# RWKV-style attention with a gated MLP: key transposes issued with the score matmuls, the early bonus on the score diagonal, u brought to channels by one transposition, and a new order table

## The chip, the cores and the metric

The kernel runs on one core of a Trainium2 chip. The metric is the time of one execution on the device in microseconds (us); less is better. Engines are named as in the profile: PE is the matmul engine (TensorE), PEld its weight loads, DVE is VectorE, ACT ScalarE, POOL GpSimd, and SP the engine that issues the DMAs. PSUM is the memory that PE writes to, in banks of 128 partitions by 512 floats.

## The reference

Batch 4, 8 heads, 768 steps, head size 48, all float32. A recurrent attention feeds a gated MLP:

```python
for t in range(S):                        # attention, state is [B, H, 48, 48]
    cur = einsum('bhd,bhe->bhde', u[None] * k[:, :, t], v[:, :, t])
    y[:, :, t] = einsum('bhd,bhde->bhe', r[:, :, t], state + cur)
    state = w[:, :, t][..., None] * state + einsum('bhd,bhe->bhde', k[:, :, t], v[:, :, t])
x = y.transpose(0, 2, 1, 3).reshape(B, S, 384)
h = maximum(x @ w_in, 0)                  # [4, 768, 1024]
u_, v_ = h[..., :512], h[..., 512:]       # v_ is normalised over its 512 columns
gated = u_ * (einsum('ts,bsd->btd', w_spatial, v_n) + b_spatial[None, :, None])
out = gated @ w_out                       # [4, 768, 384]
```

The term with u is called the bonus: step t adds v(t) times the sum over d of r(t,d) u(d) k(t,d), so it is a diagonal term of the score matrix.

## The kernel before

The attention is cut into 24 slots (4 batches by 6 chunks of 128 steps). A slot holds all 8 heads as 4 groups of two heads: head j of a group sits on partitions 64j to 64j+47, so tiles of k and r are 112 rows by 4x128 columns. A chunk has two halves of 64 steps, and the state S is carried from half to half. The steps of slot i:

- `slot_load` issues the DMAs of k, r (`kr`), w and v; `slot_prep` scales `kr` in place by products of w (scans on DVE) and makes the bonus values.
- `slot_a`: 16 score matmuls (L521), each on a 64x64 quarter of the PE array, into `paw`, two PSUM banks of which each half j of the heads has one; then a DVE `copy_predicated` (L525) puts the masked scores into the tile `AS`.
- `slot_kt`: k to time-major by 4 transpositions on the full array (L539, 112 rows by 128 columns each) into a bank of a pool of three ("pm"), and a copy of 128x448 from there to `KT` (L543, mostly on ACT).
- `slot_y`: matmuls of `AS` with v into two banks `py` (L556), and the same line with S and r.
- `slot_d`: 16 matmuls of KT with v per half (L612), on quarters of the array, into columns 256 to 447 of `paw`. The state update multiplies S on ACT (L637) or POOL and adds `paw` on DVE (L627, L625).
- `slot_x`: y is copied and added (L659, L661), transposed (L665), split in a high and a low part (L669, L672, L675) and so becomes `xT`, the MLP's input.

Bonus of the slots 0 to 5: PE makes the values per step and head (L415, `pg`), DVE multiplies v by them (L487, `bv`), and one full-array matmul with the identity starts `py` with that (L566). From slot 6 on, DVE and POOL make the values; three small copies (L493, `dgs`) and two writes (L501 on ACT, L503 on DVE or POOL) put them on the diagonal of `AS` before the scores are copied there.

The MLP multiplies in three float32r passes (high x high, high x low, low x high; L682 to L684): `ph` is x times the right half of w_in, `pu` times the left half, `pv` the mix over steps, `po` the last product. Its weights are converted by ACT and DVE as they arrive (L350, L355).

Nothing runs in the order in which it is written. Every operation is registered with `op`, and a long table of numbers (`PLAN`) gives each one its engine and a planned start; the operations are issued on each engine in the order of those starts. Lists named `hold` and `lim` give further order conditions that hold when such a table is made; they issue no instruction. While the table says that PE has a gap, before a certain operation, `fill` issues filler matmuls of a zero tile (L889, 128x128 float32, they add zero to `py`). Ten more stand at the end, while the last outputs are checked.

Of the kernel before, what the change touches and what calls it, by code (L numbers as in the profile page):

```python
# [16 lines left out]
C = 128  # L17
# [14 lines left out]
T2j S3j Tay Ad7 Ade S3oy S2on S5l Amk Voj Vqe Vse Axq Vzt Snc A1k8 V1ma V1qh V1t3 A1v4 G1y7 S9p A138 V15h V16q V1ac  # L32
A1gz V26o S2i S4k S8o Vh2 Tj4 Vax Vj2 Vk0 Vc6 Ve6 Veq Vfe Vky Vmm Ax2 Az7 V78 Vxk Tow Vu2 Tn2 Apq Tz9 T12f Tx1 V12s
A14u V1c0 T17r A19n V1cr T1eg A1fx T1he A1ig S1ao A2ar V2ep V2iz V2lm A2q1 V2ta Sod A1q3 V1s6 V1us V23b A25c V2hb S25b
A2ir V2kp V2na V2qo A2ve V2xs S3jg A40k G430 S15d A32n V3ol S4ch A4tr V4xq S2po A46i V4na S3yl A4uw V4wf S4gl A58z
V5cd S4ej A50e V51w S4ox A5i9 G5lb S2f5 A45d V4bs S57i A5xp G627 S58j A5jz G64u S4y2 A5el G5nz S2d2 A388 V3ae V3ca
V3ho A4bd V50c S2nm A3ar V4d3 V4ek V4g7 A4z9 V54h S2e3 V4b2 V4du V4hi V4l8 A52m V582 S47l V4ki V4mk V4z1 V55s A57t
V5b2 T1sb T21v T29d A2cd A2f4 A2fr S6m S7n Smb Guu T140 Vpg Vyv V11i Vvv Gy9 V12g V13i G12l G1dr A1ji A1oc V7u V1e2
T1kb V1n7 A1d3 T16b A1ap T1nc T1pg T1fg V1j7 A1lu V1p0 T1qq A1sw V1wg T1y5 A1zs T219 A28c T2cb T2e8 T2gl A2kc A2n8
A2t6 Sla Saq S14c V18n T1aq G1c6 V1h2 V1i9 V1fe V1i0 V1jx V1kl G1jc G1nd G21l A1wk V1xs T1w7 V21i A1x9 T1mg A1ro T1zh  # L40
T244 T1v5 V20s A21u V2ca T25d A27a V29a T2b9 A2e1 T2g4 A2ho T2l1 T2my T2ou A2ri A2v4 A2wu A2yv G2zm V3c3 V3hg V3iz
G3kn G3la G3lx A3rf A3z5 V40x A3od A3te G3xh V49s A4dl V4ol S12r S19o S1rd V250 T272 G1wm V28d G29g V1z3 G22e V2by
V2d0 G2bt V2fm A31x A2a2 V2am T2r3 V34l A2nj T2k5 A2m1 T2ii T37i T2sf V2wn A2zf V33u T38r A3d4 V3g5 T3hz A3jm T3l7
# [173 lines left out]
def kernel(  # L217
# [182 lines left out]
    def slot_prep(i):  # L400
# [72 lines left out]
        for n in range(2):  # L473
# [571 lines left out]
```

## Time and profile before

| | |
|---|---|
| median of 3 runs | 362.88 us (359.57 to 364.05) |
| profiled execution | 362.92 us, of which the span of the trace 361.1 us |
| mean granted TensorE clock | 0.991 of full speed |
| busy share of the span | PE 99%, PEld 92%, DVE 75%, ACT 58%, POOL 39% |
| chain of waits that ended last | PE 92%, DVE 4%, ACT 3% |
| DMA | 47.8 MB, mean 132 GB/s |

The trace is one profiled execution. A row of a timeline has a start and a duration, both in us from the start of the span. PE is pipelined: the recorded durations of consecutive matmuls overlap, so what a matmul costs in a full stretch is the distance from its start to the next start, not its duration. A float32 matmul leaves two records, so x32 is 16 matmuls. The granted clock is given in parts of full speed (2.4 GHz); 0.5 is the lower level, 1.2 GHz.

### The profile page before, as it was taken

Reading aid. Unit: us, or ns where it says so; the run is one execution under the profiler, and the core shown is the slowest. Engines: PE = TensorE matmul, PEld = TensorE weight load, DVE = VectorE, ACT = ScalarE, POOL = GpSimd, SP = SyncE. Lnnn points to the kernel's source line nnn. Section 1 sums busy time; section 2 is a strip of 40 time slices with the busy share of each in tenths; the row PEclk is TensorE's granted clock in tenths of the full one; section 3 lists DMA queues with packets and bytes.
Section 4 is the critical chain, followed back from the end, with each engine's and each line's share of the span. In section 5 each row is a group of like instructions: output and inputs, shape, how many; then the busy total and the mean of one; then the engine's idle time right before and its main releaser. Section 6 shows DMA issues by size and latency. Waiting matters only on the chain.

```text
span 361.1 us, 11353 instructions
## 1 busy us (share of the span) xinstructions
PE 356.2 (99%) x4656; PEld 331.1 (92%) x4656; DVE 271.3 (75%) x596; ACT 211.1 (58%) x587; POOL 141.1 (39%) x187
## 2 busy tenths in 40 slices
PE   7999999999999999999999999999999999999998
PEld 7987898899899989899999899899999888999997
DVE  8789998999999878999898697788565667333140
ACT  2357999896573777784454478783632296512212
POOL 1344357105544653526631267437335322223110
PEclk9978999999999999999999999999999999999999
DMA  7971976961554657634453643433545010000011
GB/s 201 262 224 56 274 247 178 287 220 49 147 142 132 209 159 230 174 84 149 144 159 118 186 146 117 121 99 107 142 129 168 1 25 2 22 23 0 24 65 71
DMA packets 21545, 47.80 MB, mean 132 GB/s; under 512 B 2545, under 2 KB 10354, under 8 KB 21490
## 3 DMA queue, kind: packets, MB, share of 16 engines
q1 hardware_dynamic: 21346, 46.85, 44.1%
q8 instruction: 37, 0.61, 0.7%
q14 instruction: 18, 0.15, 0.1%
q10 hardware_dynamic: 144, 0.20, 0.1%
HBM read 42.32 MB, written 4.72 MB: 130 GB/s over the span
## 4 chain that ended last, share of the span: by engine, by line
PE 92%; DVE 4%; ACT 3%; issue 1%; POOL 0%; DVEq 0%
PE pv L682 9%; PE pv L684 8%; PE pv L683 8%; PE py L556 7%; PE ph L682 5%; PE ph L684 5%; PE pu L682 5%; PE ph L683 5%; PE py L889 4%; PE pu L684 4%; PE po L682 4%; PE pu L683 4%; PE po L684 4%; PE po L683 4%; PE paw L521 4%; PE paw L612 3%
## 5 line engine op out<-in xcount | busy, mean ns | idle before, releaser
L682 PE MATMUL pv<-ws,vh 128*128 128x384 f32 x192 | 65.6, 342 | 0.0
L684 PE MATMUL pv<-ws,vl 128*128 128x384 f32 x192 | 64.3, 335 | 0.0
L683 PE MATMUL pv<-ws,vh 128*128 128x384 f32 x192 | 64.3, 335 | 0.0
L788 DVE TENSOR_TENSOR t<-pv,b_sb 128x384 f32<-128x384 f32 x32 | 17.6, 552 | 29.9 <-PE pv L684 29.9
L682 PEld LDWEIGHTS pv<-ws,vh 128*128 128x128 f32 x192 | 36.1, 188 | 0.5
L683 PEld LDWEIGHTS pv<-ws,vh 128*128 128x128 f32 x192 | 36.1, 188 | 0.2
L684 PEld LDWEIGHTS pv<-ws,vl 128*128 128x128 f32 x192 | 36.0, 188 | 0.0
L792 ACT CAST gh<-t 128x384 fp32r<-128x384 f32 x32 | 15.9, 509 | 32.2 <-DVE t L790 31.2
L682 PE MATMUL pu<-xT,wi 128*128 128x384 f32 x96 | 34.0, 354 | 0.1
L682 PE MATMUL po<-wo,gh 128*128 128x384 f32 x96 | 33.2, 346 | 0.0
L684 PE MATMUL pu<-xT,wi 128*128 128x384 f32 x96 | 32.4, 338 | 0.0
L684 PE MATMUL po<-wo,gl 128*128 128x384 f32 x96 | 32.3, 337 | 0.0
L683 PE MATMUL po<-wo,gh 128*128 128x384 f32 x96 | 32.3, 336 | 0.0
L683 PE MATMUL pu<-xT,wi 128*128 128x384 f32 x96 | 32.2, 336 | 0.0
L793 POOL TENSOR_TENSOR gl<-t,gh 128x384 fp32r<-128x384 f32 x14 | 14.7, 1053 | 44.4 <-ACT gh L792 44.2
L637 ACT ACTIVATE S<-S,prod 112x48 f32<-112x48 f32 x100 | 25.2, 323 | 9.3 <-DVE S L627 7.2
L711 ACT ACTIVATE hv<-ph 128x512 f32<-128x512 f32 x24 | 14.3, 594 | 27.7 <-PE ph L684 27.5
L682 PE MATMUL ph<-wi,xT 128*128 128x512 f32 x72 | 29.4, 409 | 0.0
L684 PE MATMUL ph<-wi,xT 128*128 128x512 f32 x72 | 28.3, 393 | 0.0
L683 PE MATMUL ph<-wi,xT 128*128 128x512 f32 x72 | 28.3, 392 | 0.0
L754 POOL TENSOR_TENSOR vl<-hv,vh 128x512 fp32r<-128x512 f32 x14 | 18.1, 1300 | 25.2 <-ACT vh L752 24.9
L779 ACT ACTIVATE us<-pu 128x384 f32<-128x384 f32 x32 | 15.1, 486 | 14.7 <-PE pu L684 14.6
(199 smaller groups left out, 964.7 us busy)
## 6 DMA issues: line engine op xcount, KB each, us to landing
kr<-in_tr_dram SPq DMA_DIRECT2D x24, 448.0 KB, 4.8
N<-in_nat_dram SPq DMA_DIRECT2D x18, 384.0 KB, 3.4
Nw<-in_gt_dram SPq DMA_DIRECT2D x16, 384.0 KB, 3.4
W<-in_tr_dram SPq DMA_DIRECT2D x24, 225.8 KB, 3.4
v<-in_nat_dram SPq DMA_DIRECT2D x24, 192.0 KB, 3.8
out_dram<-ot SPq DMA_DIRECT2D x18, 192.0 KB, 3.3
wst<-in_w_spT_dram SPq DMA_DIRECT2D x12, 192.0 KB, 4.9
out_dram<-ot SPq DMA_DIRECT2D x10, 96.0 KB, 3.5
```

What stands on the lines that cost most here:

```text
L521: nc.tensor.matmul(pa()[ks, j, g * L:(g + 1) * L], kr()[rs, 0, ts_], kr()[rs, 1, ts_], start=True, stop=True)
L556: nc.tensor.matmul(py()[row][L * a:L * (a + 1), D * n:D * (n + 1)], x, z, start=(a, row) not in started, stop=not left[0], skip_group_chec ...
L637: e.mul(S1[i % 2][a][:, g, :], S0[:, g, :], Wc[:, g:g + 1])
L682: nc.tensor.matmul(ps, ah, bh, start=first, stop=False)
L683: nc.tensor.matmul(ps, ah, bl, start=False, stop=False)
L684: nc.tensor.matmul(ps, al, bh, start=False, stop=last)
L754: lambda e, hv=hv, vh=vh, vl=vl: e.tensor_tensor(vl(), hv(), vh().bitcast(F32), ALU.subtract),
L779: op({"A": act(HT, True)}, lambda: nc.scalar.activation(us(), pu()[:, :HT], AF.Relu), r=[(pu, 0)], w=[(us, 0)])
L788: op({"V": dve(HT)}, lambda: nc.vector.tensor_tensor(t1(), pv()[:, :HT], b_sb[:, tsl], ALU.add), r=[(pv, 0), ("b", 0)], w=[(t1, 0)])
L792: op({"A": act(HT)}, lambda: nc.scalar.copy(gh(), t1()), r=[(t1, 0)], w=[(gh, 0)])
L793: op({"G": pool(HT), "V": dve(HT)}, lambda e: e.tensor_tensor(gl(), t1(), gh().bitcast(F32), ALU.subtract), r=[(t1, 0), (gh, 0)], w=[(gl, ...
L889: nc.tensor.matmul(pw, zk, zk, start=False, stop=True, skip_group_check=True)
```

## The change

1. The transpositions of k move into the score operation: after the 16 scores, 8 transpositions of 48 rows by 128 columns, one per group and head, write into columns 256 to 447 of the same two banks `paw`, which the state products of that slot overwrite later. The separate operation `slot_kt` is gone; KT is now 128x384. The score operation therefore waits also for the state adds of the slot before, which read those columns. The state products take 48 rows throughout.
2. Slots 0 to 5 get their bonus as the later ones do, by three copies and two writes on the diagonal of `AS`; `bv`, its matmul with the identity, two clearings of `AS` and one of `py` go.
3. u comes as 4x128 and is brought to channels by one transposition, not by 8 matmuls of one column.
4. The conditions in `hold` and `lim` go, the filler's start value changes, and the table is new. It has 58 fillers where there were 45.

```diff
 PLAN = """
-T2j S3j Tay Ad7 Ade S3oy S2on S5l Amk Voj Vqe Vse Axq Vzt Snc A1k8 V1ma V1qh V1t3 A1v4 G1y7 S9p A138 V15h V16q V1ac
+T1x9 S3j Thi Aik Aid S3n0 S4xw S5l Amk Vq8 Vsu Vwf Ayg G11s Spe A1l5 V1pd V1sw V1uw A1x6 V1yz Smb A15y V19x V1b6 V1ej
...
@@ slot_prep
-        if i < B_PE:
-            if i < AB:
-                op({"G": 0.5, "V": 0.3}, lambda e: e.memset(As(), 0.0), w=[(As, 0), (As, 1)], port=True)
-            bv = q["bv"] = buf(pm, [P, DM], "w3", f"bv{i}", W3)
-            op({"V": 0.56}, lambda: nc.vector.tensor_tensor(
-                bv().rearrange("p (h d) -> p h d", d=D), v().rearrange("p (h d) -> p h d", d=D),
-                dg()[:, :H].unsqueeze(2).broadcast_to([P, H, D]), ALU.mult), r=[(dg, 0), (v, 0)], w=[(bv, 0)])
-            return
@@ slot_a
+        pd = q["pd"] = buf(psA, [P, 2, 512], "pd", f"pd{i}", 1)
+        pd.make = lambda: paw
+        KT = q["KT"] = buf(p2, [P, 2, G * D], "KT", f"KT{i}", 1)
...
+            for g in range(G):
+                for j in range(2):
+                    rs = slice(64 * j, 64 * j + D)
+                    nc.tensor.matmul(pd()[:, j, G * L + g * D:G * L + (g + 1) * D], kr()[rs, 0, g * C:(g + 1) * C],
+                                     ident[rs, rs], is_transpose=True, start=True, stop=True)
...
-        op({"T": 0.53}, mm, r=[(kr, "k"), (kr, "r")], w=[(pa, 0)], mode="64x64")
+        op({"T": 0.73}, mm, r=[(kr, "k"), (kr, "r"), ("ds", i - 1)], w=[(pa, 0), (pd, 0)], mode="64x64")
+        op({"A": 0.53, "V": 0.56}, lambda e: (e.copy if e is nc.scalar else e.tensor_copy)(
+            KT(), pd()[:, :, G * L:G * L + G * D]), r=[(pd, 0)], w=[(KT, 0)])
@@ slot_kt
-            for g in range(G):
-                nc.tensor.transpose(pt()[:, g, :], kr()[:, 0, g * C:(g + 1) * C], ident[:R, :R])
-        op({"T": 0.317}, tp, r=[(kr, "k"), ("ds", i - 1)], w=[(pm_, 0)])
-        op({"A": 0.53, "V": 0.62},
-           lambda e: (e.copy if e is nc.scalar else e.tensor_copy)(KT(), pt()), r=[(pm_, 0)], w=[(KT, 0)])
@@ slot_y
-                nc.tensor.matmul(py()[0][:, :DM], ident, bv(), start=True, stop=False, skip_group_check=True)
-            op({"T": 0.67}, bonus, r=[(bv, 0)], w=[(py, 0)])
-        elif i == B_PE:
-            op({"V": 0.42}, lambda: nc.vector.memset(py()[0][:, :DM], 0.0), w=[(py, 0)])
@@ slot_d
-                    rows = slice(64 * j, 64 + j * D)
+                    rows = slice(64 * j, 64 * j + D)
...
-                        nc.tensor.matmul(pa()[rows, a, G * L + g * D:G * L + (g + 1) * D], KT()[ps, g, rows],
+                        nc.tensor.matmul(pa()[rows, a, G * L + g * D:G * L + (g + 1) * D], KT()[ps, j, g * D:(g + 1) * D],
                                          v()[ps, hs], start=True, stop=True)
@@ hv_unit
-        hold = lim["hv"][-4:-3]
...
-               r=[(xh, j), (xl, j)] + [("wv", k_, p) for p in range(2)] + (hold if k_ == 0 else []),
+               r=[(xh, j), (xl, j)] + [("wv", k_, p) for p in range(2)],
@@ fill
-        t = free = 1.1
+        t = free = 2.3
...
-                    warm(max(0.0, cold - 0.1) / 0.43 + max(0.0, o.start - max(b, COLD) - 0.1) / 0.224)
+                    warm(cold / 0.43 + max(0.0, o.start - max(b, COLD) - 0.1) / 0.224)
@@ u
-                nc.tensor.matmul(pu_()[64 * j:64 * j + D, g:g + 1], u_sb[:1, n * D:(n + 1) * D], ones[:1],
-                                 start=True, stop=True)
+    op({"S": 0.45}, lambda: nc.sync.dma_start(u4, gu[:G].rearrange("g p a -> g (p a)")), w=[("u4", 0)], dma=0.01)
+    op({"T": 0.1}, lambda: nc.tensor.transpose(pu_()[:, :G], u4, ident[:G, :G]), r=[("u4", 0)], w=[(pu_, 0)])
```

How the order of the instructions moves is shown at three places. Numbers behind a tile's name count buffers; an x behind a row counts equal neighbours.

PE at the start of the program, before (`py` from `zk` is the filler, `pu__` is u, `pg` the bonus values, `pt` the transposed k, `paw` the scores and the state products):

```order
L889 MATMUL py0_88<-zk_78 128x128 x7
L931 MATMUL pu__167<-few_97,u_sb_110 48x1 x8
L889 MATMUL py0_88<-zk_78 128x128 x5
L415 MATMUL pg0_192<-up_sb_111,rk0_184 128x2 x4
L889 MATMUL py0_88<-zk_78 128x128
L539 MATMUL pt0_207<-ident_92,kr0_144 128x112 x4
L889 MATMUL py0_88<-zk_78 128x128
L521 MATMUL paw_87<-kr0_144 64x64 x16
L889 MATMUL py0_88<-zk_78 128x128 x10
L612 MATMUL paw_87<-v0_154,KT0_235 64x48 x2
```

PE at the same place, changed:

```order
L852 MATMUL py0_88<-zk_78 128x128 x9
L890 MATMUL pu__171<-ident_92,u_sb_110 128x4
L852 MATMUL py0_88<-zk_78 128x128
L415 MATMUL pg0_177<-up_sb_111,rk0_160 128x2 x4
L852 MATMUL py0_88<-zk_78 128x128 x5
L516 MATMUL paw_87<-kr0_143 64x64 x16
L522 MATMUL paw_87<-ident_92,kr0_143 128x48 x8
L852 MATMUL py0_88<-zk_78 128x128 x8
L587 MATMUL paw_87<-v0_151,KT0_238 48x48 x16
L415 MATMUL pg1_275<-up_sb_111,rk1_246 128x2 x4
L852 MATMUL py0_88<-zk_78 128x128 x9
```

The transpositions now follow the scores at once, the copy to KT lies under 8 fillers, and the bonus values of slot 1 come before the outputs of slot 0.

PE in the middle of the program at slot 12, before (`ph` and `pu` are MLP products):

```order
L684 MATMUL ph1_5_2513<-wi0_122,xT1_1_1_2362 128x512
L539 MATMUL pt12_2535<-ident_92,kr12_2209 128x112 x4
L682 MATMUL pu1_1_0_2544<-xT1_1_0_2353,wi0_122 128x384
L683 MATMUL pu1_1_0_2544<-xT1_1_1_2362,wi0_122 128x384
L684 MATMUL pu1_1_0_2544<-xT1_1_0_2353,wi1_123 128x384
L521 MATMUL paw_87<-kr12_2209 64x64 x16
L612 MATMUL paw_87<-v12_2337,KT12_2550 64x48 x2
```

PE at slot 12, changed, the scores with what follows and then the state products with what stands around them:

```order
L659 MATMUL po0_1_2_2454<-wo0_126,gl0_1_3_1868 128x384
L516 MATMUL paw_87<-kr12_2250 64x64 x16
L522 MATMUL paw_87<-ident_92,kr12_2250 128x48 x8
L543 MATMUL py0_88<-v11_2230,AS1_86 64x48
...
L659 MATMUL pu1_0_3_2556<-xT1_0_0_1879,wi1_123 128x384
L587 MATMUL paw_87<-v12_2440,KT12_2543 48x48 x16
L640 MATMUL yt11_2594<-ident_92,y11_2551 128x128 x3
```

Before, the state products (L612) stand right behind the scores in 13 of the 24 slots, both on quarters of the array. Now the copy to KT has to come between them, so the state products stand by themselves between full-array matmuls, and the array changes its split more often: counted in the order of PE from the second transposition of y (of slot 1) to the end, 50 times before and 104 times in the change.

ACT near the start, before:

```order
L937 COPY up_sb_111<-pu__167 48x4 x2
L350 ACTIVATE e_('wv', 0)_203<-d_('wv', 0)_146 128x512
L543 COPY KT0_235<-pt0_207 128x448
L476 COPY vs0_270<-v0_154 64x192
L355 CAST wi0_122<-e_('wv', 0)_203 128x512
L476 COPY vs0_270<-v0_154 64x192
L350 ACTIVATE e_('wv', 2)_303<-d_('wv', 2)_156 128x512
L637 ACTIVATE S101_116<-S0_114,prod_131 112x48 x4
L659 COPY y0_337<-py0_88 128x384
```

ACT at the same place, changed:

```order
L893 COPY up_sb_111<-pu__171 48x4 x2
L485 COPY dgs0_186<-pg0_177 128x4
L350 ACTIVATE e_('wv', 0)_190<-d_('wv', 0)_145 128x512
L485 COPY dgs0_186<-pg0_177 64x4
L493 ACTIVATE AS0_85<-id64_105,dgs0_186 128x64 x4
L526 COPY KT0_238<-paw_87 128x384
L493 ACTIVATE AS0_85<-id64_105,dgs0_186 128x64 x4
L355 CAST wi0_122<-e_('wv', 0)_190 128x512
L476 COPY vs0_281<-v0_151 64x192
```

The copies and the writes on the diagonal of slot 0 (L485, L493) stand on ACT among the conversions of the weights, and those of slots 1 and 2 follow behind them in the same way.

## Rows read from the trace of the kernel before

**Rows 1.** The page: span, busy time of each engine, chain of waits by engine.
```profile
span 361.1 us, 11353 instructions
PE 356.2 (99%) x4656; PEld 331.1 (92%) x4656; DVE 271.3 (75%) x596; ACT 211.1 (58%) x587; POOL 141.1 (39%) x187
PE 92%; DVE 4%; ACT 3%; issue 1%; POOL 0%; DVEq 0%
```

**Rows 2.** Windows: busy of PE, PEld, DVE, ACT, POOL; PEclk, DMA share, GB/s.
```profile
25.00:30.00 5.00, 5.00 (x75) 4.11 (x75) 3.80 (x9) 3.89 (x11) 2.33 (x3) 0.61 0.13 51
30.00:60.00 30.00, 30.00 (x602) 25.14 (x595) 28.45 (x61) 27.24 (x77) 15.31 (x20) 1.00 0.68 202
```

**Rows 3.** Timeline of PE from its first filler to the transposition of y of slot 1.
```profile
2.34 3.35 PE L889 MATMUL py<-zk 128*128 128x128 f32 x14 [2.34 <-DVE py L279]
...
6.70 2.50 PE L889 MATMUL py<-zk 128*128 128x128 f32 x10
8.99 1.71 PE L415 MATMUL pg<-up_sb,rk 112*128 112x2 f32 x8
...
12.46 1.13 PE L521 MATMUL paw<-kr 48*64 48x64 f32 x32
13.53 3.32 PE L889 MATMUL py<-zk 128*128 128x128 f32 x20
...
32.64 0.55 PE L665 MATMUL yt<-ident,y 128*128 128x128 f32 x3
```

**Rows 4.** Timeline of DVE, slot 0's product of k and r.
```profile
6.94 0.67 DVE L410 TENSOR_TENSOR rk<-kr 112x512 f32<-112x512 f32 x1
```

**Rows 5.** Groups of ACT by line: busy us, mean ns of one, idle before.
```profile
L637 ACT ACTIVATE S<-S,prod 112x48 f32<-112x48 f32 x100 | 25.2, 323 | 9.3 <-DVE S L627 7.2 <-DVE S L625 2.0
L501 ACT ACTIVATE AS<-id,dgs 128x64 f32<-128x64 f32 x68 | 17.9, 337 | 3.4 <-DVE dgs L493 2.5 <-PE py L556 0.8
...
L543 ACT COPY KT<-pt 128x448 f32<-128x448 f32 x22 | 11.6, 528 | 12.5 <-PE pt L539 12.5
L476 ACT COPY vs<-v 64x192 f32<-64x192 f32 x27 | 9.4, 351 | 3.4 <-DMA v<-in_nat_dram 2.9
L659 ACT COPY y<-py 128x384 f32<-128x384 f32 x16 | 7.6, 476 | 7.6 <-PE py L556 7.5
...
L493 ACT COPY dgs<-dg 64x4 f32<-64x4 f32 x16 | 3.1, 192 | 1.8 <-DVE dg L467 1.6
```

**Rows 6.** Timeline of ACT, a conversion beside four state products.
```profile
26.57 0.67 ACT L350 ACTIVATE e_('wv', 1)_398<-d_('wv', 1)_212 128x512 f32<-128x512 f32 x1
27.14 0.99 ACT L637 ACTIVATE S<-S,prod 112x48 f32<-112x48 f32 x4
```

**Rows 7.** Timeline of PE, the bonus matmul of an early slot between its neighbours.
```profile
39.64 0.40 PE L682 MATMUL ph<-wi,xT 128*128 128x512 f32 x1
...
40.33 0.81 PE L566 MATMUL py<-bv,ident 128*128 128x384 f32 x2
40.97 0.55 PE L539 MATMUL pt<-ident,kr 112*128 112x112 f32 x4
```

**Rows 8.** Timeline of PE in the middle, around the scores of one slot.
```profile
199.20 0.33 PE L683 MATMUL pv<-ws,vh 128*128 128x384 f32 x1
199.37 0.34 PE L684 MATMUL pv<-ws,vl 128*128 128x384 f32 x1
199.64 0.26 PE L556 MATMUL py<-v,AS 64*64 64x48 f32 x2
...
200.61 0.66 PE L521 MATMUL paw<-kr 48*64 48x64 f32 x32
201.09 0.63 PE L612 MATMUL paw<-v,KT 64*64 64x48 f32 x32
201.65 0.60 PE L539 MATMUL pt<-ident,kr 112*128 112x112 f32 x4
202.02 0.42 PE L682 MATMUL pv<-ws,vh 128*128 128x384 f32 x1
```

More of the change, by code (lines that the diff above doesn't have):

```diff
@@ L600, in slot_d @@
         KT, v = q["KT"], q["v"]
-        pa = q["pd"] = buf(psA, [P, 2, 512], "pd", f"pd{i}", 1)
-        pa.make = lambda: paw
+        pa = q["pd"]
         subs = 1 if i % NC_ == NC_ - 1 else SUB
@@ L687 @@
     gg = {}
-    lim = {"hv": [], "out": []}
     def hv_unit(b, c):
@@ L739, in scale @@
         small({"V": 0.16, "G": 0.2}, lambda e: e.tensor_tensor(part(5), part(7), part(1), ALU.mult), 1, 7, 5)
-        for j, (hv, end) in enumerate(zip(hvs, done)):
+        for j, hv in enumerate(hvs):
             vh, vl = vn[b, h * NH + j] = tuple(
@@ L754, in scale @@
                lambda e, hv=hv, vh=vh, vl=vl: e.tensor_tensor(vl(), hv(), vh().bitcast(F32), ALU.subtract),
-               r=[(hv, 0), (vh, 0)], w=[(vl, 0), end], port=True)
+               r=[(hv, 0), (vh, 0)], w=[(vl, 0)], port=True)
     def g_unit(b, h, f):
@@ L770, in g_unit @@
                + ([(us, 1)] if k_ == 0 else []), w=[(pu, 0)])
-        hold = [(vn[b, NC_ - 1][0], 0)]
-        if f > 0:
-            hold += lim["out"]
-        if f == KF - 1:
-            lim["out"] = []
-        if f == 0:
-            hold += [("wo", k_, 1) for k_ in range(KF)] if h else []
         op({"A": act(HT, True)}, lambda: nc.scalar.activation(us(), pu()[:, :HT], AF.Relu),
@@ L785, in g_unit @@
                 k_ == 0, k_ == NC_ - 1),
-               r=[(vh, 0), (vl, 0)] + [("ws", p, k_, h) for p in range(2)]
-               + (hold if k_ == 0 else []), w=[(pv, 0)])
+               r=[(vh, 0), (vl, 0)] + [("ws", p, k_, h) for p in range(2)],
+               w=[(pv, 0)])
         op({"V": dve(HT)}, lambda: nc.vector.tensor_tensor(t1(), pv()[:, :HT], b_sb[:, tsl], ALU.add),
@@ L803, in out_unit @@
                 po()[:, :DM], gh()[:, ts_], gl()[:, ts_], wo[0][:, f, :], wo[1][:, f, :], f == 0, f == KF - 1),
-               r=[(gh, 0), (gl, 0)] + [("wo", f, p) for p in range(2)]
-               + ([(gg[b, h, KF - 1][1], 0)] if f == 0 else []), w=[(po, 0), ("po", b, h, j)])
-        lim["out"].append(("po", b, h, j))
+               r=[(gh, 0), (gl, 0)] + [("wo", f, p) for p in range(2)],
+               w=[(po, 0)])
         op({"A": act(DM, True), "V": dve(DM)},
@@ L864, in general @@
             with tc.For_i(0, B, 1) as n:
-                lim["hv"], lim["out"] = [], []
                 prog.reset()
@@ L923 @@
     op({"T": 0.1}, lambda: warm(1), w=[("pw", 0)])
[L924 removed]
+    u4 = u_sb[:G, :P]
+    op({"S": 0.45}, lambda: nc.sync.dma_start(u4, gu[:G].rearrange("g p a -> g (p a)")), w=[("u4", 0)], dma=0.01)
     pu_ = buf(psM, [P, 512], "pm", "pu_", 3)
[L927 to L934 removed]
+    op({"T": 0.1}, lambda: nc.tensor.transpose(pu_()[:, :G], u4, ident[:G, :G]), r=[("u4", 0)], w=[(pu_, 0)])
     for j in range(2):
@@ L948 @@
             slot_w(i, 0)
-        slot_kt(i)
         slot_y(i)
```

190 lines of the change are left out of this document (86 added, 104 removed).

## The prediction

> **What bounds the kernel now.** I read the page first: PE is busy 99% of the span of 361.1 us and holds 92% of the chain of waits [rows 1]. Busy time alone would not prove it, since records of pipelined matmuls overlap, but the windows agree: from 30 to 60 us PE is busy for 30.00 of 30.00 us, while ScalarE has 27.24 and VectorE 28.45 [rows 2]. So from about 26 us on PE is issued without a gap, and what it is given to do sets the end; ScalarE and VectorE are close behind it as long as the attention runs. Before that, PE is carried along by fillers: its timeline from 2.34 us shows blocks of them between the first steps of the slots [rows 3], and there the other engines set the pace. I therefore read the start as a chain of waits, and the rest as a ledger of PE time by distances from start to start. The border is the second transposition of y (slot 1), at 32.64 us before [rows 3].
>
> The profiled execution took 362.92 us, 1.8 us over its span, and the median is 362.88; so the sum is made against 362.92 and needs no correction. About 2% (7.3 us: 355.6 and 370.1) is what a measurement of this kernel can tell from no change.
>
> **The start.** Fillers at first cost 3.35 / 7 = 0.48 us each, later ones 3.32 / 10 = 0.33 [rows 3]. In the changed order of PE: 9 fillers from 2.34 end at 6.7; u transposed, two tenths at most, 6.9; one filler, 7.4. The bonus values of slot 0 wait for the product of k and r, which VectorE ends at 6.94 + 0.67 = 7.6 [rows 4], and take 1.71 [rows 3]: 9.3. Five fillers, 11.7; scores 1.13 [rows 3], 12.9; the 8 transpositions at about half of that, 13.4. Eight fillers of 0.33 (2.7) cover the copy to KT, which costs ScalarE 0.53 [rows 5]: 16.1. State products 201.65 - 201.09 = 0.56 [rows 8], and the bonus values of slot 1 at 1.71 x 0.33 / 0.48 = 1.2: 17.8.
>
> From there ScalarE is the slow one, since it now writes diagonals among conversions. Up to the second transposition of y its order holds 4 groups of state products of 0.99 [rows 6] (4.0), 3 groups of diagonal writes of 4 x 0.337 less overlap (17.9 / 17 = 1.05 each [rows 5], 3.2), 6 copies of y, xT and KT at 0.48 to 0.53 (3.0), 4 copies of v at 0.35 (1.4), 5 conversions at 0.67 at most [rows 6] (3.3) and 6 small copies of 0.19 [rows 5] (1.1): 16.0. Neighbours overlap, 0.67 becoming 27.14 - 26.57 = 0.57 [rows 6]; a tenth for each of the 28 pieces would make it 13.3. I take 14.8, the middle: 32.6; then y's add on VectorE, half a us by the copy of the same shape (0.476 [rows 5]): 33.1. **Term 1: +0.5.** The transposition of u, the loads and the smaller set of clearings lie beside this and cost nothing; were they uncovered they could not move more than the 0.2 already counted.
>
> **The ledger from there on.**
> - **Term 2, moved ahead: -1.4.** Of the three MLP products of the first `ph` only one stood before the border; now all three do. One costs 40.33 - 39.64 = 0.69 [rows 7]; two of them, 1.4.
> - **Term 3, bonus matmuls: -2.6.** Four of six lie behind the border, at 40.97 - 40.33 = 0.64 [rows 7].
> - **Term 4, old transpositions: -7.8.** 21 slots at 202.02 - 201.65 = 0.37 [rows 8].
> - **Term 5, new transpositions: +5.0.** No row shows a transposition on half the rows. Bounds: if the two heads of a group run beside each other and only the 48 moving columns count, 4 x (0.37 / 4) x 48 / 112 = 0.16 a slot; if the eight run one after another at the old price of a load of 128 columns, 8 x 0.37 / 4 = 0.74. The nearest rows are the scores: 16 in 201.09 - 200.61 = 0.48 [rows 8], on the same rows of the array, straight ahead of them; two of those four quarters' columns make one such half, so a pair goes for two scores, 0.06. Four pairs: 0.24; times 21.
> - **Term 6, changes of the array's split: +4.9.** Behind the border the order has 54 more of them. From quarters to the full array costs 0.56 (state products with what follows) less 0.48 (scores with what follows) = 0.08; from full to quarters 199.64 - 199.37 = 0.27 less 199.37 - 199.20 = 0.17, so 0.10 [rows 8]. Bounds 0 (a change between halves and quarters may be free, none is shown) and 0.11; I take 0.09 for all. 54 x 0.09.
> - **Term 7, fillers: -1.0.** Three fewer behind the border, 0.33 each.
> - **Term 8, ScalarE behind the border: +1.0.** Slots 3 to 5 add to it one group of diagonal writes (1.05) and nine small copies (9 x 0.19 = 1.7), together 2.8, where it was idle for 30.00 - 27.24 = 2.76 [rows 2]. VectorE loses three products of v at about half a us and takes the other writes, about even. I put a third of the 2.8 on the path; bounds 0 and 2.8.
>
> The state products keep their number and lose only rows, which I price at zero: scores of 48 rows and 64 columns go at 0.48 for 16, state products of 64 rows at no more than 0.56 with the change of split behind them [rows 8]. Dropped conditions issue nothing. Sum: +0.5 - 1.4 - 2.6 - 7.8 + 5.0 + 4.9 - 1.0 + 1.0 = **-1.4**, so 362.9 - 1.4 = **361.5 us**. In words: what the removed operations give back, the split of the array takes again.
>
> **A rule that speaks against it.** The trace's old transpositions take 0.37 / 4 = 0.0925 each [rows 8]. The Trainium skill, "TensorE: Matmul & The Clock Gate", section "LDWEIGHTS", says that a load costs by its columns and not by its rows, P / 1.2 ns. By that, eight loads of 128 columns one behind the other would take 0.85 us a slot, and the sum would come out about 13 us higher; the trace's 0.0925 lies under the page's 0.107, and no row here shows two halves loaded side by side. The Trainium skill, "TensorEngine Tiling (Array Packing)", section "Key Properties", says that a change of tiling mode drains the engine; the 0.08 and 0.10 of rows 8 agree for quarters and full array, and no row shows halves against quarters.
>
> **Rivals.**
> - **R1, slower: the two halves do not run beside each other.** Then a slot pays 0.74 in place of 0.24, and 21 x 0.50 = 10.5 more: 372.0. It decides from 0.65 a slot on. For it: a load of 128 columns is the longest part of such a transposition, and PEld is busy 331.1 us [rows 1]. Against: scores with the same rows run four at a time. Chance 0.08.
> - **R2, faster: the split changes for nothing and pairs cost by their moving columns.** Minus 4.9, minus 21 x 0.08 = 1.7: 354.9. For it: the 0.08 and 0.10 are differences of single starts and may hold waits for operands. Against: they agree with each other. Chance 0.12.
> - **R3: ScalarE holds the attention up.** The start at 16.0 (+1.2) and all of the 2.8 on the path (+1.8): 364.5. For it: 27.24 of 30 us; against: VectorE and POOL take some of the writes, and PE has MLP work in hand. Chance 0.14.
> - **R4: the scores wait for the adds of the slot before**, since they now write their columns, and PE, which goes in order, stands with all MLP work behind them. If each of 21 slots stands for the length of a copy of 0.35 [rows 5], 7.3: 368.8. Against: the order puts MLP products between adds and scores. Chance 0.05.
>
> The forecast itself has 0.61, with a range of its own of 358.5 to 364.5 (terms 1, 6 and 8 at either bound move it by about 3). The granted clock was 0.61 from 25 to 30 us [rows 2]: at full speed elsewhere, that is 3.9 us at the lower level and 2 us of work lost; whether it comes again or goes lies within this range, since ScalarE sets that stretch. The range of 8 in 10 is 355.0 to 368.0: it leaves out R1 (0.08), half of R2 and of R4, and little else. Faster by over 2%: R2 and a tail, 0.13. Slower by over 2%: R1 and a tail, 0.09. Within: 0.78.
>
> **What would show it.** In the changed trace: eight transpositions 0.24 us from first start to the next operation's, less the change of split (term 5; 0.6 and more is R1); state products with about 0.1 to the neighbours on both sides (term 6; no gap is R2); the second transposition of y at 33 us (term 1); ScalarE without idle time between 18 and 33 us, and PE without a gap after 33 (a gap in front of scores is R4, one in front of matmuls of `AS` is R3). The forecast is wrong if the transpositions cost what the old ones did, or if PE is idle for more than 3 us in all behind the border.

## The result

The changed kernel takes 366.80 us in the median of 4 runs (364.94 to 369.47), the kernel before, run beside it, 362.56. The ratio is 1.0122, with a 95% interval of 1.0077 to 1.0167: slower by about 1%. The forecast was 361.5 us. Repeated twice, the comparison gave 1.0099 (1.0058 to 1.0140) and 1.0165 (1.0090 to 1.0239). All ratios here leave out runs more than 1.5% above the fastest run of the same kernel. The profiled execution took 365.9 us with a span of 364.2, 3.1 us more than the span before [rows 1].

The page of the changed kernel; the lines answer to rows 1:

```profile
span 364.2 us, 11570 instructions
PE 354.3 (97%) x4751; PEld 327.2 (90%) x4751; DVE 265.8 (73%) x585; ACT 224.9 (62%) x638; POOL 127.7 (35%) x174
PE 88%; ACT 7%; DMA 2%; DVE 1%; issue 1%; POOL 0%; DVEq 0%; ACTq 0%
```

PE is less busy and the span is longer, so time went where PE does nothing. The windows of the changed kernel, columns as in rows 2:

```profile
20.00:25.00 5.00, 5.00 (x53) 4.89 (x52) 1.50 (x4) 4.48 (x15) 1.74 (x2) 0.50 0.97 292
25.00:30.00 5.00, 5.00 (x120) 4.43 (x120) 5.00 (x10) 3.69 (x13) 3.70 (x3) 0.88 0.45 105
30.00:60.00 30.00, 28.84 (x535) 23.96 (x533) 27.31 (x62) 28.11 (x86) 11.09 (x18) 1.00 0.77 227
```

From 20 to 25 us the granted clock is 0.50, the lower level, and from 30 to 60 PE is idle for 1.16 us, where it had no gap before.

PE's timeline of the start; an "issue" in brackets is time in which the engine waited for nothing the profile shows:

```profile
17.18 0.50 PE L516 MATMUL paw<-kr 48*64 48x64 f32 x17
19.00 0.46 PE L516 MATMUL paw<-kr 48*64 48x64 f32 x15 [1.32 <-issue]
19.38 0.66 PE L522 MATMUL paw<-ident,kr 48*128 48x48 f32 x8
...
32.95 0.52 PE L640 MATMUL yt<-ident,y 128*128 128x128 f32 x3
```

In the middle of slot 1's scores PE stands for 1.32 us. The matmuls on either side are of one operation, so no other engine can be waited for; the clock falls at 19.4 us. ScalarE's timeline shows who waited for it:

```profile
16.05 2.01 ACT L493 ACTIVATE AS<-id,dgs 128x64 f32<-128x64 f32 x8
20.09 0.48 ACT L526 COPY KT<-paw 128x384 f32<-128x384 f32 x1 [2.02 <-PE paw L522]
```

Last, the end. These are the sequencer rows of the line with the last branch (past it lies the path for inputs out of range); behind the duration in ns (least, median, most) stands the start in us. First the changed kernel, then the kernel before:

```profile
L942 DVEq COMPARE_BRANCH  x1: 84/84/84, 359.4 to 359.4; - x1
L942 DVEq EVENT_SEMAPHORE  x1: 21/21/21, 363.2 to 363.2; - x1
```

```profile
L987 DVEq COMPARE_BRANCH  x1: 84/84/84, 358.3 to 358.3; - x1
L987 DVEq EVENT_SEMAPHORE  x1: 21/21/21, 358.9 to 358.9; - x1
```

VectorE's next instruction behind the branch comes 3.7 us later (359.48 to 363.17), where it had been 0.5. The span ends 1.0 us after the later of VectorE's instruction and PE's last matmul, so now 3.26 us behind that matmul (360.92), not 1.03 (360.07): 2.2 of the 3.1 us.

### The profile page after: what moved, and what is told of

Read it like the earlier page. It is cut to its first block, busy times and chain, and to the rows that moved or that the text cites. A ratio compares the mean times of both kernels' runs of the same rounds, so it can differ in the third digit from the quotient of the medians.

```text
span 364.2 us, 11570 instructions
## 1 busy us (share of the span) xinstructions
PE 354.3 (97%) x4751; PEld 327.2 (90%) x4751; DVE 265.8 (73%) x585; ACT 224.9 (62%) x638; POOL 127.7 (35%) x174
## 4 chain that ended last, share of the span: by engine, by line
PE 88%; ACT 7%; DMA 2%; DVE 1%; issue 1%; POOL 0%; DVEq 0%; ACTq 0%
PE pv L657 10%; PE pv L659 9%; PE pv L658 9%; PE py L543 6%; PE py L852 5%; PE po L659 4%; PE po L658 4%; PE po L657 4%; PE ph L657 4%; PE pu L657 4%; PE pu L658 4%; PE ph L659 4%; PE pu L659 4%; PE ph L658 4%; PE paw L516 4%; PE paw L587 3%
## 5 line engine op out<-in xcount | busy, mean ns | idle before, releaser
L657 PE MATMUL po<-wo,gh 128*128 128x384 f32 x96 | 32.4, 338 | 0.0
L658 PE MATMUL po<-wo,gh 128*128 128x384 f32 x96 | 32.3, 336 | 0.0
L612 ACT ACTIVATE S<-S,prod 112x48 f32<-112x48 f32 x84 | 21.2, 326 | 6.9 <-DVE S L602 6.8
L493 ACT ACTIVATE AS<-id,dgs 128x64 f32<-128x64 f32 x92 | 24.1, 339 | 0.2
L452 POOL TENSOR_TENSOR kr<-kr,F 112x496 f32<-112x496 f32 x16 | 18.0, 1126 | 13.4 <-DVE kr L442 11.7
L852 PE MATMUL py<-zk 128*128 128x128 f32 x116 | 19.9, 325 | 2.6 <-DVE py L279 2.3
```

The costliest lines, as they stand in the source:

```text
L452: op({"V": 0.68, "G": 1.07}, lambda e: e.tensor_tensor(seg(kr()[:, 0])[:, :, :L2 - 1], seg(kr()[:, 0])[:, :, :L2 - 1], F()[:, :, 1:].unsqu ...
L493: e.mul(As()[:, j, g, :], id64, dgs()[:, j, g:g + 1])
L612: e.mul(S1[i % 2][a][:, g, :], S0[:, g, :], Wc[:, g:g + 1])
L657: nc.tensor.matmul(ps, ah, bh, start=first, stop=False)
L658: nc.tensor.matmul(ps, ah, bl, start=False, stop=False)
L852: nc.tensor.matmul(pw, zk, zk, start=False, stop=True, skip_group_check=True)
```

## The experiments

**The same kernel again, without the branch, and with transpositions in quarters.** The first kernel is the changed one, unedited. In the next two, made of the changed kernel and of the kernel before, the branch, the hint that belongs to it and the slow path are left out:

```diff
-    rv = nc.values_load(bad[0:1, 0:1], min_val=0, max_val=1)
-    with tc.If(rv > 0, label="tail"):
-        general()
```

> The changed kernel once more, nothing edited. Three theories of its +3.0 us (profiled 365.9 against 362.9): (T) the tail, 2.2 us, since VectorE stood 3.7 us between the last branch and its next instruction where it had stood 0.5 before; (S) the changes of the array's split, which with the new transpositions cost 11.2 us where I had 9.9; (W) waits in which PE is idle, 1.7 us more behind the second transposition of y. If T belongs to the program, this trace shows the 3.7 us again and the ratio is 1.010 to 1.014; if T was chance, the last PE record ends at about 361 again but the span ends 1 us after it, and the ratio falls to 1.002 to 1.008. S and W expect the same PE sums as before within 0.3 us.

Measured: 1.0099; 3.3 us behind the branch again, the span 2.9 us behind PE's last matmul. So the tail belongs to the program. But the second transposition of y came at 35.28 us; PE had stood twice, 0.96 us at 18.2 us and then 2.05 us:

```profile
24.87 0.39 PE L543 MATMUL py<-S,kr 48*64 48x48 f32 x11
27.31 0.88 PE L543 MATMUL py<-S,kr 48*64 48x48 f32 x21 [2.05 <-issue]
```

> The changed kernel without the last branch and what lies behind it (the slow path for inputs out of range is left out; the check value is computed and not read). T expects the span to end 1 us after the last PE record, so 362 us, 364 in all, 2.2 less than the changed kernel; S and W expect no more than the branch's own 0.3 us to go.

> The kernel before, with the same branch and slow path left out. Its engines all passed the branch within 0.6 us and its end waits for PE's last fillers, so T expects 0 to 0.4 us less than the kernel before. Then the changed kernel without branch against this one shows the change without the tail: T 1.002 to 1.005, S and W as sole causes 1.012.

Measured, against the kernel before: the changed kernel 1.0066 (1.0039 to 1.0092) without the branch, the kernel before 0.9980 (0.9951 to 1.0009). Both spans end 0.9 to 1.2 us behind PE's last matmul. Between them the change is still 0.9% slower, where T alone wanted 0.2 to 0.5%: the tail is a part, not the whole. The traces of this pair agree: the second transposition of y is 1.6 us later (31.91 for 30.28), from there to PE's last product it takes 0.8 us more (326.15 for 325.32), and the end adds 0.3. Leaving the branch out took 2.4 us off the changed kernel's median (365.45 for 367.82, over all runs) and 0.3 off that of the kernel before (362.50 for 362.84). That is what T wants, but resampling the runs puts the 2.4 anywhere from -0.7 to 3.8 (95%), so the times alone do not prove it.

The fourth kernel has the transpositions in quarters:

```diff
             for g in range(G):
-                for j in range(2):
-                    rs = slice(64 * j, 64 * j + D)
-                    nc.tensor.matmul(pd()[:, j, G * L + g * D:G * L + (g + 1) * D], kr()[rs, 0, g * C:(g + 1) * C],
-                                     ident[rs, rs], is_transpose=True, start=True, stop=True)
+                for a in range(SUB):
+                    for j in range(2):
+                        rs = slice(64 * j, 64 * j + D)
+                        nc.tensor.matmul(pd()[a * L:(a + 1) * L, j, G * L + g * D:G * L + (g + 1) * D],
+                                         kr()[rs, 0, g * C + a * L:g * C + (a + 1) * L],
+                                         ident[rs, rs], start=True, stop=True)
```

> The changed kernel with the transpositions cut to quarters of the array: 16 products with the identity of 48 rows by 64 columns each, in the split in which the scores run, so that between scores and transpositions nothing changes. S expects the scores' sum behind the second transposition of y to fall from 13.3 back to 11.1 us (0.10 a slot), and the products to take 0.36 (scores' 0.48 by 48/64 columns) plus 0.08 for the change to the full array, 0.44 a slot for 0.38: a net of -0.9 us, ratio 1.009 to 1.011. If the longer score sum is not the change of split but waits for the columns of the slot before, it stays at 13.3 and the time rises by 1.3 us.

Measured: 1.0192 (1.0161 to 1.0224), a miss of the time; that ratio rests on three of six runs, and the median of all six is 373.57 us, 10.7 above the kernel before. Summed behind the border from start to next start, the scores fell as S said, to 10.6 us from 13.3, but the transpositions cost 10.5 for 7.95, 0.50 a slot where S had 0.44, so nothing was won or lost there. The rest is waits: the border came at 36.30 us for 32.95, and behind it PE waited 6.3 us for 2.85. PE stood inside one operation again, now at other places and longer; the longest stand lies ahead of the border:

```profile
26.44 0.61 PE L523 MATMUL paw<-ident,kr 48*64 48x48 f32 x26
31.02 0.38 PE L523 MATMUL paw<-ident,kr 48*64 48x48 f32 x6 [3.97 <-issue]
```

Counted in PE's records (loads, matmuls and semaphores), these stands lie in the changed kernel before records 449, 705, 1473, 1985 and 5569, in this one before 450, 962, 1729, 5058 and 9409: each within 1 of 449 plus a multiple of 256. A DMA queue that the profile calls "instruction" moves 38 packets of 16 KB, about one for every 256 of PE's 9,574 records, and PE goes on 2.3 to 2.8 us after the last of them has started (once 3.2). Both point to PE standing for its code, and a denser program, with 1,152 records more, stands longer; at most of the 36 such places of a trace it does not stand. Two waits that the profile puts down to nothing don't fit the count, 0.69 and 0.89 us before record 1448 in two kernels with clearings (below), at the start of a slot's scores; they too end 2.3 to 2.5 us after such a packet has started.

The Trainium skill, "Runtime: NRT & Kernel Launch", section "Instruction fetch mechanics", says that code is refilled in 16 KiB blocks of 256 instructions, and that crossing a block is mostly hidden. The trace agrees on the 256; that it is hidden holds for PE in the kernel before, whose four traces (two of them of its variants) show no such stand above 0.15 us (its variant with the bonus alone, below, has two), and fails for the changed kernel. At record 449 the clock may be part of the difference: those four traces reached the full clock only at 15.3 to 17.3 us (one had it for 3.4 us before), every trace with a stand there had it by 8 us, and the two kernels below that got it at 15.4 and 18.8 us have none. It isn't enough by itself, since two more below had it by 7.3 us and don't stand there.

**Where the last branch lies in VectorE's code.** Clearings of one element at about 348 us, where VectorE is idle; 16 or 40 of them in the changed kernel, 8 in the kernel before:

```diff
             nc.vector.tensor_tensor(okr[:, 0:1], okr[:, 0:1], okr[:, 1:2], ALU.min)
+            for _ in range(16):
+                nc.vector.memset(over[:1, :1], 0.0)
```

> The changed kernel with 16 one-element clearings more on VectorE, at about 348 us, where VectorE is idle; they only move the last branch in VectorE's code from its 704th instruction to the 720th. Theory T in its sharper form: where VectorE's last branch lies against the blocks in which code is loaded decides whether it stands 0.5 or 3.5 us behind it. T expects the 0.5 us back, the span to end 1.0 to 1.2 us after PE's last record, and 2 us less than the changed kernel: ratio to the kernel before 1.004 to 1.008. If the stall belongs to something else of the changed kernel (its work at the end, its outputs), it stays at 3.3 to 3.7 us and the ratio at 1.010 to 1.012.

> The kernel before with 8 such clearings, which put its last branch on VectorE's 704th instruction, as in the changed kernel. T expects VectorE to stand 3.3 to 3.7 us behind the branch here too, and 2 us more: ratio 1.005 to 1.006. The rival expects 0.5 us and a ratio of 1.000.

The rows of the branch, with 16 in the changed kernel, then with 8 in the kernel before:

```profile
L944 DVEq COMPARE_BRANCH  x1: 84/84/84, 361.1 to 361.1; - x1
...
L944 DVEq EVENT_SEMAPHORE  x1: 21/21/21, 361.7 to 361.7; - x1
```

```profile
L989 DVEq COMPARE_BRANCH  x1: 84/84/84, 358.8 to 358.8; - x1
...
L989 DVEq EVENT_SEMAPHORE  x1: 21/21/21, 362.6 to 362.6; - x1
```

The stall follows the position: 0.5 us with the branch as VectorE's 694th, 696th, 700th, 720th or 744th instruction, 3.2 to 3.7 as the 704th, in all seven traces that have it there, of either kernel and its variants. In those seven a second "instruction" queue, of 8 KB packets, moves one more packet 0.6 us after VectorE has gone on (at 363.76 us in the first); no other trace with the branch has one there. 704 is also the last number ahead of 449 plus 256, a place where PE stands; that VectorE's code is cut at the same numbers is not tested. The same section of the Trainium skill says that a taken branch whose target is not in the two blocks at hand stalls until it is loaded; the trace fits that, with 3.2 to 3.7 us as the price. The kernel before with the stall ran at 1.0036 (0.9992 to 1.0079), near the 1.005 expected, but no change is not excluded. The changed kernel without it ran at 1.0188 (1.0138 to 1.0237), which T does not explain, so it ran twice more:

> The changed kernel with the 16 clearings on VectorE once more. Its tail was 1.0 us as T wanted, but its time was 1.019 of the kernel before, where T alone wants 1.004 to 1.008; its trace showed PE without code for 1.25 us at 17.6 us and a granted clock of half for 10 us right behind, and again at 48.6 us (0.69 us) and half for 3.4 us behind. Theory C: PE's code comes in blocks of 256 instructions; where the changed kernel runs through one faster than the next arrives, PE stands, and a stand is followed by a stretch at the lower clock; how long both last differs from run to run. C expects 1.004 to 1.012 in the mean of more runs, and in this trace stands only at PE's instructions 449, 705, 961 and so on in steps of 256. If the 1.019 belongs to the program, it comes again.

> The changed kernel with 40 clearings on VectorE at about 348 us, so that its last branch is the 744th instruction. T expects 0.5 us behind that branch and, in the same call, 1.5 to 2.5 us less than the changed kernel: 1.004 to 1.008. If it comes out at 1.012 or above again, as the kernel with 16 clearings did, then what the tail saves is lost ahead of it, in the start.

> The changed kernel a third time, beside the next kernel on the same chip. Open: whether the 2 us of the tail, plain in every trace, are in the times, and how much of the rest is the start. T expects 1.010 to 1.012 here and 3.3 to 3.7 us behind VectorE's last branch; C expects PE to stand at its instruction 449 if the full clock came before 10 us, and a stretch at half behind it.

Measured: 1.0121, 1.0132 and, for the unshifted kernel, 1.0165. The first misses what C wanted of its trace too: no stand at 449, only the 0.89 us before record 1448. Pooled, 18 runs with the short tail and 19 with the long one have the same median, 367.6 and 367.7 us. In the three traces of each, the tail is 2.0 us shorter (1.02 for 3.08), but the last product of PE comes 2.2 us later (361.4 for 359.1), with a stretch at the lower clock at about 50 us in all three of the shifted kernels and in none of the three unshifted:

```profile
45.00:50.00 5.00, 4.63 (x96) 3.65 (x96) 4.96 (x13) 4.86 (x19) 1.76 (x3) 1.00 0.85 242
50.00:55.00 5.00, 5.00 (x42) 4.86 (x41) 4.34 (x11) 4.90 (x14) 2.27 (x4) 0.66 0.83 254
55.00:60.00 5.00, 5.00 (x87) 4.45 (x85) 3.60 (x9) 3.36 (x9) 2.13 (x8) 1.00 0.94 294
```

In two of the three PE also waits 2.21 and 1.63 us for xT at about 154 us (at most 0.37 in the unshifted). In VectorE's order the add for xT stands behind a reduction that waits for POOL; from the second trace with 16 clearings:

```profile
152.53 0.55 DVE L467 TENSOR_REDUCE dg<-N 128x8 f32<-128x384 f32 x1 [1.10 <-POOL N L465]
153.00 0.55 DVE L652 TENSOR_TENSOR xT<-yt,xT 128x384 fp32r<-128x384 f32 x1
153.61 0.50 PE L657 MATMUL ph<-wi,xT 128*128 128x512 f32 x1 [2.21 <-DVE xT L652]
```

Neither belongs to the clearings alone: without them, the changed kernel without branch waits 1.43 us for the same xT, and the kernel with seven operations on POOL (below) has a stretch at half at 53 us; the kernel with later loads (below) has the clearings and neither. What causes this loss stays open. That the tail holds 2 us of each trace is shown; that clearings which take it away make this kernel faster is not.

**Loads issued later.** The 16 clearings, and four words of the table (two parts of w_in, two of w_spatial):

```diff
-Spe S1bz S1e2 S1f3
+S1a4 S1s6 S1uo S1uy
```

> The same, with four loads issued later by the table alone: the last third of w_in's right half behind W of slot 3 (from 9.4 to about 17 us), one third of its left half behind k and r of slot 4, two parts of w_spatial behind W of slot 4. Between 10 and 26 us the queues carry 0.5 to 0.9 MB less. Theory C1, that the code blocks come late because these loads are ahead of them: no stand of PE above 0.3 us before 30 us, the second transposition of y at 31.3 us as in the run that had no stand, and 1.5 to 3 us less than the kernel without this edit. C2, that a block needs its 2.3 to 2.7 us however empty the queues are: the stand of 0.7 to 1.3 us at instruction 449 stays, and the time too (within 0.7 us, or more if the weights now come late).

Measured: 1.0135 (1.0073 to 1.0198), beside 1.0121 without the edit. Its trace has no stand before 30 us but the border at 33.17 us, later than C1's 31.3, and one stretch of 3.4 us at half; at 25.5 us PE waits 1.18 us for a state product of ScalarE. C1 is not borne out in time; since stands also differ between runs of one kernel, C2 is not refuted by one trace.

**Seven operations on POOL instead of ScalarE.** Words of the table (A is ScalarE, G is POOL): five state products, two diagonal writes, and the product of k and r that is put earlier:

```diff
-A1mq A1ql A1ym A22x A2sz A2gt A30l G24o
+G1mq G1ql G1ym G22x G2sz G2gt G30l G1ya
```

> The changed kernel with seven operations of the slots 1 to 4 on POOL and not on ScalarE, by the table alone: five state products (1.0 us each on ScalarE, 0.5 on POOL) and two diagonal writes (1.06 against 0.6 to 1.1); POOL's product of k and r of slot 3 is put ahead of two of them. ScalarE has 7 us less to do between 22 and 46 us, in which it had no idle time but 1 us. Theory A, that ScalarE paces this stretch and so makes half of the missing 2.4 us behind the second transposition of y and of the late start: 1.5 to 4 us less than the changed kernel, ratio 1.000 to 1.007. If PE's own work or its code loading sets the stretch, the ratio stays at 1.009 to 1.012.

Measured: 1.0088 (1.0054 to 1.0122). Its branch is VectorE's 700th instruction, so its tail is short as well, and beside the shifted kernels it is faster by 0.3 to 1%. But the trace's border is at 36.35 us, where PE waits 1.63 us for VectorE's add of y, with the full clock only from 18.8 us on. Inconclusive: ScalarE may pace this stretch, the time doesn't prove it.

**Transpositions twice.** The loop of the 8 transpositions is written twice:

```diff
+            for g in range(G):
+                for j in range(2):
+                    rs = slice(64 * j, 64 * j + D)
+                    nc.tensor.matmul(pd()[:, j, G * L + g * D:G * L + (g + 1) * D], kr()[rs, 0, g * C:(g + 1) * C],
+                                     ident[rs, rs], is_transpose=True, start=True, stop=True)
```

> The changed kernel with the 8 transpositions of a slot issued twice, one look for PE's prices. Behind the second transposition of y the first 8 cost 7.95 us in 21 slots, 0.379 each with the change of split that follows them. S expects 8 more, without any change of split, to cost 0.28 a slot (two heads beside each other at 0.07 a pair), 5.9 us in all; by my forecast's 0.24 it is 5.0; if the eight run one after another, as the trace's 0.38 would also allow, 0.37 a slot and 7.8 us.

PE in the middle of the program, first the changed kernel, then with 16 transpositions (L527 is the second set):

```profile
204.68 0.34 PE L659 MATMUL po<-wo,gl 128*128 128x384 f32 x1
204.94 0.69 PE L516 MATMUL paw<-kr 48*64 48x64 f32 x32
205.57 0.45 PE L522 MATMUL paw<-ident,kr 48*128 48x48 f32 x8
205.95 0.26 PE L543 MATMUL py<-v,AS 64*64 64x48 f32 x2
```

```profile
205.70 0.69 PE L516 MATMUL paw<-kr 48*64 48x64 f32 x32
206.33 0.45 PE L522 MATMUL paw<-ident,kr 48*128 48x48 f32 x8
206.61 0.41 PE L527 MATMUL paw<-ident,kr 48*128 48x48 f32 x8
206.95 0.26 PE L548 MATMUL py<-v,AS 64*64 64x48 f32 x2
```

The second set adds 13.16 - 7.95 = 5.2 us in 21 slots, 0.248 each: the forecast's 0.24. The halves do run beside each other. What is dear stands around them: 0.63 from scores to transpositions where scores took 0.48 [rows 8], and 0.38 in all for transpositions that cost 0.25.

**Transpositions ahead of the scores.** The two loops of the operation change places, so that the same lines stand ahead of the scores:

```diff
         def mm():
+            for g in range(G):
+                for j in range(2):
...
+                                     ident[rs, rs], is_transpose=True, start=True, stop=True)
             for g in range(G):
                 for a in range(SUB):
```

> The changed kernel with the 8 transpositions ahead of the 16 scores in the same operation. What follows the operation runs on quarters of the array in 15 of 24 slots, as the scores do, so those slots change the split once less. S expects scores and transpositions together to fall from 21.2 us behind the second transposition of y to 19.7 to 20.2, with 0.10 us for each change saved, and the time by 1 to 1.5 us (1.006 to 1.009); if the 0.10 behind the scores is not a change of split but PE's price of the first transposition, the sum stays at 21.2.

```profile
209.07 0.45 PE L513 MATMUL paw<-ident,kr 48*128 48x48 f32 x8
209.45 0.69 PE L521 MATMUL paw<-kr 48*64 48x64 f32 x32
209.97 0.21 PE L543 MATMUL py<-v,AS 64*64 64x48 f32 x2
```

Scores with what follows on quarters of the array take 0.52 for 0.63, and the sum of both falls from 21.2 us to 19.5 (transpositions 7.97, scores 11.5): the 0.10 is the change of split. Behind the border the split now changes 94 times for 104, and from the border to PE's last product it took 324.0 us for 325.1 to 325.5 in three traces of the changed kernel. The ratio was 1.0075 (1.0027 to 1.0123), beside 1.0165 for the changed kernel, but it rests on 6 of 12 runs; over all runs the medians are 367.21 and 368.06 us, so the gain of 1 us is shown in the trace and not in the time. Its border came at 37.67 us without a stand above 0.2 us before it; its first scores took 1.13 us, as in rows 3, and later ones 0.69, so it seems to have had the lower clock early on.

**The early bonus alone, in the kernel before.** The table's words of `bv` give way to three copies and two diagonal writes, and the gap of the bonus matmul stays empty in the plan, so that no fillers enter it:

```diff
-                nc.tensor.matmul(py()[0][:, :DM], ident, bv(), start=True, stop=False, skip_group_check=True)
-            op({"T": 0.67}, bonus, r=[(bv, 0)], w=[(py, 0)])
+            op({"T": 0.67}, lambda: None)
```

> The kernel before with one part of the change alone: the bonus of slots 0 to 5 on the diagonal of the scores. Transpositions, u, fillers and the rest of the order are those of before; ScalarE writes slot 0, POOL the diagonals of slots 1 to 5, ScalarE makes the small copies of slots 0 to 2 and VectorE those of 3 to 5. The ledger gives PE back 4 x 0.64 us behind the second transposition of y, and two more bonuses ahead of it: 2 to 3.5 us less, ratio 0.990 to 0.995, if PE is the bound there. If the writes on the diagonal come late (POOL in order behind its products of k and r), copies of the scores wait and it is 1.000 or above.

Measured: 1.0044 (1.0009 to 1.0079): no gain, rather a loss. The border came at 30.54 us, but from there to PE's last product it took 326.15 us for 324.58. The four matmuls behind the border are gone (2.77 us), but PE is idle there for 3.9 us where it was 1.2, and its other work takes 1.6 us more from start to start. PE's waits, over the whole program:

```profile
PE yt L650 <- DVE y L646: 1.3, 2, 0.8
PE py L549 <- issue: 1.1, 2, 0.8
PE yt L657 <- ACT xT L654: 0.9, 2, 0.6
```

The time that PE was given back goes in good part into waits for y and xT, which VectorE and ScalarE make, and into two stands of 0.33 and 0.75 us at the places of the code blocks.

**The start of the kernel before, once more.**

> The kernel before, one look more at its start: the second transposition of y came at 32.6 us in its first trace, with the full clock from 15.3 us on, where the changed kernel had it at 32.9 with the full clock from 5.7 us. C expects no stand of PE for code above 0.3 us in the first 60 us here, whenever the full clock comes, and 30 to 32.7 us for that transposition.

```profile
20.00:25.00 5.00, 4.67 (x74) 3.97 (x71) 4.67 (x9) 2.47 (x8) 1.77 (x2) 0.91 0.61 184
25.00:30.00 5.00, 5.00 (x118) 4.07 (x114) 3.93 (x11) 4.26 (x11) 3.15 (x3) 0.75 0.28 96
```

No stand, the border at 32.22 us, and 3.4 us at the lower clock. The first trace of this kernel had 6.8 us of it, its variants with clearings and without branch 3.4 in this stretch; all three traces of the changed kernel had 6.8.

## Why the prediction was wrong

- **Term 1, the start: +0.5 forecast.** (The border is the second transposition of y.) The profiled pair gave +0.3, as if right, but by luck; over more traces it is mis-sized. The border lies at 32.95, 35.28 and 33.49 us in the changed kernel (mean 33.9), at 32.64 and 32.22 before, and at 32.25 and 30.28 in its variants with clearings and without branch (mean 31.8): +2.0, or +1.5 between unedited traces alone. Part of that is the base: 32.64 was the latest border of the kernel before, and my 33.1 lies 0.8 under the changed kernel's mean. All three traces of the changed kernel show stands of 1.0 to 1.5 us at PE's record 449 (one a second of 2.05), then 6.8 us at half clock. The chain of waits that I added up had neither. But the stands don't settle it: two kernels with clearings have no stand before the border and reach it at 33.16 and 33.17 us, and the changed kernel without branch stands for 0.68 us and reaches it at 31.91. Nor does the clock fall only behind a stand: it fell in the kernel before at 22.1 us, and not at the first stand of the unedited repeat. What makes the start late stays open.
- **Terms 2, 3 and 4**: -1.6 (over all MLP products, for -1.4), -2.8 and -7.8 measured, as forecast. But term 3 as a gain was not there in the kernel with the bonus alone: the PE time came back, in good part as waits.
- **Term 5**: +5.2 for +5.0, right. R1 fell, and so did the rule by which eight loads stand in a row (0.85 a slot).
- **Term 6, the changes of split: +4.9 forecast, about 6.2 measured.** Transpositions 7.95 less 5.2, scores 13.28 less 11.10, y's transpositions 7.22 less 6.23, the rest 0.3. About 0.115 each, not 0.09, and 0.13 behind the halves, which no row before had shown. R2 fell.
- **Term 7**: -0.4 for -1.0: a filler at full speed is cheaper than the 0.33 I took.
- **Term 8**: PE's waits behind the border rose by 1.7 us for +1.0. Three of them, 1.7 us in all, ended with ScalarE:

```profile
PE yt L640 <- ACT us L744: 0.8, 1, 0.8
PE pv L657 <- ACT us L744: 0.7, 1, 0.7
PE pu L657 <- ACT dgs L485: 0.2, 1, 0.2
```

  So it is R3's engine, but not R3's place: no wait stands in front of the matmuls of `AS`, and none in front of scores, where R4 had it.
- Terms 2 to 8 made -1.9; measured, from the border to PE's last product, 325.12 - 324.58 = **+0.5**.
- **The end: nothing forecast, +2.2 in the profile.** I had put everything behind PE's last matmul down as equal, 1.8 us outside the span included. The step that failed is the first one: that PE is issued without a gap and "what it is given to do sets the end". It left out what follows the last matmul, where VectorE waits 3.7 us behind its branch for 0.5.

Added up by the traces' means: +2.0 at the start, +0.3 behind the border (325.2 less 324.9 over the same traces), +2.0 at the end, 4.3 us, against 4.2 in the medians of the first comparison. The choice of traces moves the parts: unedited ones alone give +1.5, +0.6 and +2.0; with the changed kernel's own variants without branch and with clearings taken in as well, the start is +1.9 and the stretch behind the border +1.3. The forecast of 361.5 missed all three, in the same direction. The end alone does not turn the sign: without the branch the change is still 0.9% slower where I had it 0.4% faster, so terms 1, 6, 7 and 8 failed in size as well, and of the start only the size is known. None of the changed kernel's versions beats the kernel before.

## What to carry to other kernels

A ledger of PE's time is worth what the other engines leave of it: check each gain against who must deliver next, as the bonus alone showed. Price what lies behind the last matmul too: VectorE's branch cost 0.5 us in one kernel and 3.7 in the other. Small matmuls in a row seem to cost code as well as array time, so count PE's instructions per microsecond where a change packs them. Group operations by the array's split, and put the odd one where its neighbour has the same. Where one run of each kernel is read, a start whose clock and code come as they like can hide or feign 2 us.

## What the runs showed that was not expected

- Where PE stands inside an operation, it is at one of every 256 of its records: 0.2 to 4.0 us, most often where only attention matmuls follow each other. At most of these places it doesn't stand.
- The last branch costs VectorE 0.5 us or, at one of the six places tried, 3.2 to 3.7, in whichever kernel.
- A change between quarters of the array and halves costs 0.10 to 0.13 us, as much as one to the full array.
